# First batch's gate and value from the plain 512-wide read, and weight units in a three-step pipeline with the integer add on DVE

## The chip, the cores and the metric

The kernel runs on one core of a Trainium2 chip. The metric is the device time of one execution in microseconds (us). The engines are named as in the profile: PE is TensorE (matmuls), DVE is VectorE, ACT is ScalarE, POOL is GpSimd, SP is SyncE, which here only issues DMAs. Each engine works its own list of instructions strictly in order and waits on semaphores for the others.

## The reference, cut to what matters

```python
scale = 1.0 / np.sqrt(D)                                        # B, H, S, D = 8, 8, 512, 64; Ns = 32
a = softmax(scale * x @ state.T)                                # per head, over the 32 state rows
xread = a @ state
a2 = softmax(scale * state @ x.T)                               # per head, over the 512 rows
sread = a2 @ x
t = concat([xread, sread])                                      # 8 batches of 512 + 32 rows, 512 wide
g, val = t @ w_gate, t @ w_val                                  # 512 -> 1536
y = (g * sigmoid(g) * val) @ w_out                              # 1536 -> 512
h = y @ w2_in                                                   # 512 -> 2048
out = (h * sigmoid(1.702 * h)) @ w2_out                         # 2048 -> 512
```

## The kernel before

Every product is split in three: each operand is a high part (rounded by a cast) and a low part (the rest), and high x high, high x low and low x high are three matmuls into one PSUM tile. "xh" and "xl" are the two parts of an operand that is read from PSUM: ACT copies the high part, DVE subtracts it.

**Stages.** An opening (the word list START, worked off one word after the other) brings in batch 0's attention and the first weights. Then the blocks of the first expert layer: batches 0 to 6, the "tail" (the 8 x 32 state rows as one block, 256 wide), and batch 7, each as a loop over f = 0..11 (128 columns of the 1536). At last the second layer, nine blocks of 16 steps. All three stages are one list of instructions per engine, in the order in which the code writes them. No scheduler moves anything.

**One f of a block.** The product of the gate (PE, into a PSUM tile gv of which there are two), its sigmoid (ACT, L718), the first multiply (DVE, L720, "mult0"), the product of the value, the second multiply (DVE, L730, "mult1"), the high part of h (ACT, L736), its low part (DVE, L738), and then `out1` of the f before (12 matmuls, L679 to L681). Between them stand pieces of the next batch's attention, at places that the tables BLOCK0 (during batch 0) and GROUP (later) give by f and a place 0, 1 or 2. In all batches the gate's and the value's product goes by `state_weights` and `mm_state`: first the state times the weights of two f (per group of four heads 6 matmuls, then xh and xl of 512 columns), then the attention weights `a` times that, 6 matmuls for each gate and each value. Only the tail takes the plain product, 12 matmuls with the read rows as an operand.

**Weight units.** The weights lie in DRAM as 64-bit floats and come as "units" of 128 x 512 numbers, through four buffers `raw`. A unit is turned into 32-bit floats (`w_begin`): ACT scales the upper word into `wt` and the lower word in place (L192, L193), DVE shifts, and then joins sign and bits (L194, L195), and POOL adds the lower word as integers (L198). Then it is cut (`w_end`): ACT copies the high part (L208), POOL subtracts it (L209). Batch 0 takes 36 such units (24 for gate and value, 12 for out), the tail 4, batch 7 about 24. The out units are stored back as 32-bit floats and from batch 1 on are only cut. In batch 0 `w_beside` puts a begin or an end at five places of each f; elsewhere `need` runs as many as are wanted, with two begun at a time. All weight DMAs are issued on SP.

Of the kernel before, what the change touches and what calls it, by code (L numbers as in the profile page):

```python
# [79 lines left out]
def kernel(  # L80
# [76 lines left out]
    pos = {"dma": 0, "begun": 0, "done": 0, "ahead": 4}  # L157
# [6 lines left out]
    def w_dma(ahead=None):  # L164
        ahead = ahead or pos["ahead"]
        while pos["dma"] < pos.get("limit", len(stream)) and len(raws) + len(held) < ahead:
            key, src, _, _ = stream[pos["dma"]]
            if isinstance(src, tuple):
                raw = work.tile([P, DM], src[0].dtype, name="raw", tag="raw", bufs=RAWS)
                for n, part in enumerate(src):  # L170
                    sy.dma_start(raw[:, n * 2 * P : (n + 1) * 2 * P], part)
            elif src.dtype == F32:
                raw = work.tile([P, DM], F32, name="raw", tag="raw", bufs=RAWS)
                sy.dma_start(raw, src)
            else:
                raw = work.tile([P, DM], src.dtype, name="raw", tag="raw", bufs=RAWS)
                sy.dma_start(raw.rearrange("p (k m) -> p k m", m=src.shape[2]), src)
# [3 lines left out]
    def w_begin():  # L181
# [3 lines left out]
        key, src, _, _ = stream[pos["begun"]]  # L185
        t = raw = raws.pop(key)
        if isinstance(src, tuple) or src.dtype != F32:
# [10 lines left out]
            pool_e.tensor_tensor(tu, tu, lo, op=ALU.add)  # L198
        else:
            held.add(key)  # L200
        temps[key] = t
        pos["begun"] += 1

    def w_end():
        key, src, (pl, tag, bufs), keep = stream[pos["done"]]
        t = temps.pop(key)
        u = (pl or x2p).tile([P, 2, DM], F32R, name="wu", tag=tag, bufs=bufs)
        a.copy(u[:, 0, :], t)  # L208
        pool_e.tensor_tensor(u[:, 1, :], t, f32(u[:, 0, :]), op=ALU.subtract)  # L209
        if keep is not None:  # L210
            sy.dma_start(keep, t)
        held.discard(key)
        units[key] = u
        pos["done"] += 1

    def w_step(lead=2):
        if pos["begun"] > pos["done"]:
            w_end()
# [80 lines left out]
    class Group:  # L299


        def __init__(self, b, g, slots=None):
            self.b, self.g, self.slots = b, g, slots or {}

        def tile(self, tag, shape, dt=F32):
            if tag in self.slots:
                return wp.tile(shape, dt, name=tag, tag=self.slots[tag], bufs=1)
            return ap.tile(shape, dt, name=tag, tag={"aT": "ST", "xth1": "xth0", "xtl1": "xtl0"}.get(tag, tag))
# [12 lines left out]
        def turn(self, q):  # L321
# [6 lines left out]
            self.xt[q] = ps, self.tile(f"xth{q}", [P, S], F32R), self.tile(f"xtl{q}", [P, S], F32R)  # L328
# [515 lines left out]
```

## Time and profile before

| | us |
|---|---|
| median of 3 runs (lowest, highest) | 1674.07 (1673.71, 1675.39) |
| the profiled execution's own time | 1674.44 |
| its span on the core | 1672.7 |
| PE busy in the span | 1568.0 (94%) |
| DVE, ACT, POOL busy | 859.8, 682.1, 350.7 |

The span is what lies between the first and the last instruction; 1.7 us of the time lie around it. The share of busy time mixes stages that have different limits, so the views below are read by stretch. The rows name tiles without their buffer numbers, and an arrow in brackets says how long an engine stood idle before the instruction and whose end it waited for.

### The profile page before, as it was taken

Reading aid. Unit: us, or ns where it says so; the run is one execution under the profiler, and the core shown is the slowest. Engines: PE = TensorE matmul, PEld = TensorE weight load, DVE = VectorE, ACT = ScalarE, POOL = GpSimd, SP = SyncE. Lnnn points to the kernel's source line nnn. Section 1 sums busy time; section 2 is a strip of 40 time slices with the busy share of each in tenths; the row PEclk is TensorE's granted clock in tenths of the full one; section 3 lists DMA queues with packets and bytes.
Section 4 is the critical chain, followed back from the end, with each engine's and each line's share of the span. In section 5 each row is a group of like instructions: output and inputs, shape, how many; then the busy total and the mean of one; then the engine's idle time right before and its main releaser. Section 6 shows DMA issues by size and latency. Waiting matters only on the chain.

```text
span 1672.7 us, 18772 instructions
## 1 busy us (share of the span) xinstructions
PE 1568.0 (94%) x7100; PEld 1274.6 (76%) x7100; DVE 859.8 (51%) x1361; ACT 682.1 (41%) x1217; POOL 350.7 (21%) x263
## 2 busy tenths in 40 slices
PE   4667899999999999989987999999999999999997
PEld 2445688888888888869765888888888888888886
DVE  5788766676767666654787333232322322222222
ACT  5566554545555454544565232222222222222222
POOL 3566322222222221225686020000000000000000
PEclk7788899999999999999999999999999999999999
DMA  4445321212122212223445001010101010000000
GB/s 144 126 137 151 103 52 48 77 42 82 49 67 59 64 45 80 52 76 108 145 157 176 19 0 45 7 45 7 41 10 38 13 38 13 32 20 29 10 26 14
DMA packets 85747, 102.40 MB, mean 61 GB/s; under 512 B 44184, under 2 KB 53400, under 8 KB 85656
## 3 DMA queue, kind: packets, MB, share of 16 engines
q1 hardware_dynamic: 85656, 101.21, 20.1%
q8 instruction: 55, 0.90, 0.2%
q14 instruction: 36, 0.29, 0.1%
HBM read 79.69 MB, written 21.50 MB: 60 GB/s over the span
## 4 chain that ended last, share of the span: by engine, by line
PE 45%; DVE 4%; ACT 1%; issue 1%; DMA 0%; DVEq 0%
PE gv L236 8%; PE gv L235 8%; PE gv L234 8%; PE acc L247 7%; PE acc L246 7%; PE acc L248 7%; DVE wt L195 2%; DVE wt L194 1%; ACT wu L208 0%; ACT wt L192 0%; ACT h L736 0%; DVE sg L730 0%; DVE sg L720 0%; DVE xl L571 0%; DMA raw<-in_moe_w_in_dram 0%
## 5 line engine op out<-in xcount | busy, mean ns | idle before, releaser
L805 DVE TENSOR_TENSOR sg<-gv,sg 128x512 f32<-128x512 f32 (+1 forms) x144 | 95.3, 662 | 426.1 <-ACT sg L804 426.1
L804 ACT ACTIVATE sg<-gv 128x512 f32<-128x512 f32 (+1 forms) x144 | 82.6, 574 | 442.1 <-PE gv L236 442.1
L236 PE MATMUL gv<-xl,wu 128*128 128x512 f32 (+1 forms) x576 | 219.5, 381 | 0.0
L235 PE MATMUL gv<-xh,wu 128*128 128x512 f32 (+1 forms) x576 | 219.2, 381 | 0.0
L234 PE MATMUL gv<-xh,wu 128*128 128x512 f32 (+1 forms) x576 | 219.0, 380 | 0.0
L209 POOL TENSOR_TENSOR wu<-raw,wu 128x512 fp32r<-128x512 f32 x96 | 126.0, 1312 | 425.3 <-ACT wu L208 392.9
L247 PE MATMUL acc<-wu,h 128*128 128x512 f32 x544 | 213.2, 392 | 0.0
L246 PE MATMUL acc<-wu,h 128*128 128x512 f32 x544 | 212.9, 391 | 0.0
L248 PE MATMUL acc<-wu,h 128*128 128x512 f32 x544 | 212.1, 390 | 0.0
L241 PE MATMUL gv<-a,xh 128*128 128x512 f32 x384 | 160.6, 418 | 14.9 <-DVE sg L730 10.0
L242 PE MATMUL gv<-a,xl 128*128 128x512 f32 x384 | 157.6, 410 | 16.8 <-DVE xl L571 16.8
L679 PE MATMUL acc<-h,wu 128*128 128x512 f32 (+1 forms) x432 | 167.0, 387 | 4.8 <-ACT h L736 4.8
L680 PE MATMUL acc<-h,wu 128*128 128x512 f32 (+1 forms) x432 | 165.5, 383 | 0.9 <-POOL wu L209 0.9
L681 PE MATMUL acc<-h,wu 128*128 128x512 f32 (+1 forms) x432 | 165.2, 382 | 1.0 <-DVE h L738 0.9
L243 PE MATMUL gv<-a,xh 128*128 128x512 f32 x384 | 156.3, 407 | 0.0
L571 DVE TENSOR_TENSOR h<-sg,h 128x512 fp32r<-128x512 f32 (+1 forms) x144 | 96.4, 670 | 95.4 <-ACT h L570 90.0
L570 ACT CAST h<-sg 128x512 fp32r<-128x512 f32 (+1 forms) x144 | 86.0, 597 | 105.6 <-DVE sg L805 105.6
L234 PEld LDWEIGHTS gv<-xh,wu 128*128 128x128 f32 x576 | 108.5, 188 | 22.3
L235 PEld LDWEIGHTS gv<-xh,wu 128*128 128x128 f32 x576 | 108.2, 188 | 22.2
L236 PEld LDWEIGHTS gv<-xl,wu 128*128 128x128 f32 x576 | 108.3, 188 | 21.8
L720 DVE TENSOR_TENSOR sg<-gv,sg 128x512 f32<-128x512 f32 (+1 forms) x108 | 71.2, 659 | 95.5 <-ACT sg L718 95.1
L246 PEld LDWEIGHTS acc<-wu,h 128*128 128x128 f32 x544 | 102.1, 188 | 22.5
(105 smaller groups left out, 2728.0 us busy)
## 6 DMA issues: line engine op xcount, KB each, us to landing
raw<-w1o SPq DMA_DIRECT2D x96, 256.0 KB
raw<-in_moe_w_out_dram SPq DMA_DIRECT2D x28, 512.0 KB
y<-ev SPq DMA_DIRECT2D x16, 512.0 KB
raw<-in_moe_w_in_dram SPq DMA_DIRECT2D x16, 512.0 KB
xr<-y SPq DMA_DIRECT2D x32, 256.0 KB
out_dram<-ev SPq DMA_DIRECT2D x16, 512.0 KB
xn<-in_x_dram SPq DMA_DIRECT2D x14, 512.0 KB
raw<-in_moe_w_gate_dram SPq DMA_DIRECT2D x24, 256.0 KB
```

The costliest lines, as they stand in the source:

```text
L234: pe.matmul(ps[:, :N], wh, xh, start=k == 0, stop=False)
L235: pe.matmul(ps[:, :N], wl, xh, start=False, stop=False)
L236: pe.matmul(ps[:, :N], wh, xl, start=False, stop=k == KD - 1)
L241: pe.matmul(ps, wh, xh, start=k == 0, stop=False)
L242: pe.matmul(ps, wl, xh, start=False, stop=False)
L243: pe.matmul(ps, wh, xl, start=False, stop=k == len(pairs) - 1)
L246: pe.matmul(ps, lh, rh, start=first, stop=False)
L247: pe.matmul(ps, lh, rl, start=False, stop=False)
L248: pe.matmul(ps, ll, rh, start=False, stop=last)
L679: pe.matmul(ps, w[:, 0, c], h[:, 0, :N], start=f == 0, stop=False)
L680: pe.matmul(ps, w[:, 1, c], h[:, 0, :N], start=False, stop=False)
L681: pe.matmul(ps, w[:, 0, c], h[:, 1, :N], start=False, stop=f == F1 - 1)
```

## The change

Four things are changed. Batch 0's gate and value take the plain product: the read rows (`xread`, the softmax weights stacked as high and low part in `stk`, times the state's two parts) become the operand `xop`, and each gate and value is 12 matmuls; there is no `state_weights` in batch 0. The weight units go through a pipeline (`w_slot`): one slot turns unit n on ACT, copies the high part of a unit joined in an earlier slot, joins unit n on DVE, and subtracts the low part of the one copied. The integer add (L208 of after) is DVE's, in `w_join`, as an instruction that the listing of the order calls ISA, with 128x1024 as its shape. In batch 0 three slots stand in each f (`beside`), their subtractions in turn on POOL and on DVE; elsewhere `need` runs slots with the subtraction on POOL. The first four units' eight DMAs are issued on ACT's queue ahead of all else there. The scores of the first two groups are computed for two heads' pairs at once (`scores_wide`).

```diff
 START = """
-A0.load0 state0 A0.load1 weights1 A0.turn0 A1.load0 attn_state A0.turn_h0 A1.load1 weights2 A0.turn1
...
+weights4 A0.load0 state0 A0.load1 A1.load0 A1.load1 A0.turn0 attn_state A0.turn_h0 A0.turn_l0:v A0.turn1
+slot A0.turn_h1 A0.turn_l1:v A0.scores_wide A1.turn0 slot A0.max_n A1.turn_h0 A0.less_max:p A1.turn_l0:v
+A1.turn1 A0.exp_n A1.turn_h1 A1.turn_l1:v A1.scores_wide A0.sum_n cut_state A0.over_sum:v slot A0.back
+A1.max_n A0.stack_h0:a A0.stack_l0:v A0.stack_h1:a A0.stack_l1:v xread0 xread1 A1.less_max:v A1.exp_n slot
+xread_l0 xread_l1 A1.sum_n A1.over_sum:v A1.back A0.max_s A1.stack_h0:a A1.stack_l0:v A1.stack_h1:a
+A1.stack_l1:v xread2 xread3 slot A1.max_s xread_l2 xread_l3 G0.load A1.exp_s A0.exp_s state1
...
-    pos = {"dma": 0, "begun": 0, "done": 0, "ahead": 4}
+    pos = {"dma": 0, "turned": 0, "joined": 0, "cut": 0, "ahead": 4, "q": a}
...
+    def w_join():
+        t, hi, lo = temps[stream[pos["joined"]][0]]
+        pos["joined"] += 1
+        if hi is not None:
+            tu = t.bitcast(U32)
             v.tensor_scalar(out=tu, in0=tu, scalar1=3, scalar2=None, op0=ALU.logical_shift_left)
             v.scalar_tensor_tensor(
                 out=tu, in0=hi, scalar=0x80000000, in1=tu, op0=ALU.bitwise_and, op1=ALU.bitwise_or
             )
-            pool_e.tensor_tensor(tu, tu, lo, op=ALU.add)
...
+            v.tensor_tensor(tu, tu, lo, op=ALU.add)
+
+    def w_slot(eng=None):
+
+        if pos["turned"] < pos["dma"]:
+            w_turn()
+        key, src, (pl, tag, bufs), keep = stream[pos["cut"]]
+        ready = pos["cut"] < pos["joined"] and pos["cut"] < pos.get("cap", len(stream))
+        if ready:
+            t = temps.pop(key)[0]
+            u = (pl or x2p).tile([P, 2, DM], F32R, name="wu", tag=tag, bufs=bufs)
+            a.copy(u[:, 0, :], t)
+        if pos["joined"] < pos["turned"]:
+            w_join()
+        if ready:
+            (eng or pool_e).tensor_tensor(u[:, 1, :], t, f32(u[:, 0, :]), op=ALU.subtract)
...
     def need(key):
-        while pos["done"] <= where[key]:
-            w_step()
+        while pos["cut"] <= where[key]:
+            w_slot()
...
+    def xread(hp):
+        ps = at()
+        stk, sb = stks.pop(hp)[0], stks["state"]
+        pe.matmul(ps, sb[:, 0, hp, :], stk, start=True, stop=False)
+        pe.matmul(ps, sb[:, 1, hp, :], stk, start=False, stop=True)
+        xop[hp] = x_tiles(xp, hp, S)
+        a.copy(xop[hp][0], ps)
+        return lambda: v.tensor_tensor(xop[hp][1], ps, f32(xop[hp][0]), op=ALU.subtract)
...
+        plain = tail or i == 0
...
-            for g, place in enumerate([(F1 - 1, 1)] * 2 if tail else [(F1 - 2, 1), (F1 - 1, 0)]):
+            for g, place in enumerate([(F1 - 1, 1)] * 2 if plain else [(F1 - 2, 1), (F1 - 1, 0)]):
...
+        def beside():
+
+            if i == 0:
+                w_slot(v if pos["cut"] % 2 else pool_e)
...
             product(pg, f, 0)
+            beside()
             sg = work.tile([P, 512], F32, name="sg", tag="sg")
             a.activation(sg[:, :N], pg[:, :N], ACTF.Sigmoid)
-            w_beside("B")
             v.tensor_tensor(sg[:, :N], pg[:, :N], sg[:, :N], op=ALU.mult)
-            w_beside("E")
...
             product(pv, f, 1)
-            w_beside("B")
+            beside()
             v.tensor_tensor(sg[:, :N], pv[:, :N], sg[:, :N], op=ALU.mult)
...
                 out1(f - 1, nxt, 0) if f == F1 - 1 else out1(f - 1)
+            beside()
             run(f, 2)
```

In the listings below, L720/L730/L738 of before are L775/L784/L790 of after, L194/L195 are L204/L205, and the cut L208/L209 of before is L219/L223.

DVE in batch 0, f = 3, from mult0 to the last row before the next mult0. Before:

```order
L720 TENSOR_TENSOR sg_667<-gv_660,sg_667 128x512
L345 TENSOR_TENSOR ST_673<-at_674,ST_673 64x512
L335 TENSOR_TENSOR xtl1_685<-at_679,xth1_684 128x512
L194 TENSOR_SCALAR wt_695<-wt_695 128x512
L195 SCALAR_TENSOR_TENSOR wt_695<-raw_522,wt_695 128x512
L730 TENSOR_TENSOR sg_667<-gv_688,sg_667 128x512
L194 TENSOR_SCALAR wt_708<-wt_708 128x512
L195 SCALAR_TENSOR_TENSOR wt_708<-raw_575,wt_708 128x512
L738 TENSOR_TENSOR h_717<-sg_667,h_717 128x512
L194 TENSOR_SCALAR wt_736<-wt_736 128x512
L195 SCALAR_TENSOR_TENSOR wt_736<-raw_596,wt_736 128x512
L571 TENSOR_TENSOR xl_752<-at_744,xh_751 128x512
```

After, the same step (the slot that stands before the next mult0 with it):

```order
L775 TENSOR_TENSOR sg_680<-gv_656,sg_680 128x512
L362 TENSOR_TENSOR ST_683<-at_684,ST_683 64x512
L352 TENSOR_TENSOR xt1_694<-at_689,xt1_694 128x512
L204 TENSOR_SCALAR wt_710<-wt_710 128x512
L205 SCALAR_TENSOR_TENSOR wt_710<-raw_552,wt_710 128x512
L208 ISA wt_710<-raw_552,wt_710 128x1024
L784 TENSOR_TENSOR sg_680<-gv_697,sg_680 128x512
L790 TENSOR_TENSOR h_723<-sg_680,h_723 128x512
L204 TENSOR_SCALAR wt_738<-wt_738 128x512
L205 SCALAR_TENSOR_TENSOR wt_738<-raw_593,wt_738 128x512
L208 ISA wt_738<-raw_593,wt_738 128x1024
L223 TENSOR_TENSOR wu_741<-wt_710,wu_741 128x512
```

The three units of a step stay; each has one instruction more on DVE, every second low part is DVE's, and the low part `xl` of `state_weights` is gone.

ACT in the tail, its first two f, with the one 64-bit unit (wt_6292 before, wt_6333 after). Before:

```order
L718 ACTIVATE sg_6280<-gv_6267 128x256
L208 CAST wu_6283<-raw_6009 128x512
L192 ACTIVATE wt_6292<-raw_6286 128x512
L193 ACTIVATE raw_6286<-raw_6286 128x512
L736 CAST h_6314<-sg_6280 128x256
L718 ACTIVATE sg_6330<-gv_6317 128x256
```

After:

```order
L774 ACTIVATE sg_6288<-gv_6275 128x256
L219 CAST wu_6291<-raw_6017 128x512
L789 CAST h_6314<-sg_6288 128x256
L774 ACTIVATE sg_6330<-gv_6317 128x256
L192 ACTIVATE wt_6333<-raw_6294 128x512
L193 ACTIVATE raw_6294<-raw_6294 128x512
```

The turn of this unit stands one f later, behind h of f = 0 and the sigmoid of f = 1; on DVE its join stands likewise behind mult0 of f = 1.

ACT in batch 7, one f from sigmoid to sigmoid. Before:

```order
L718 ACTIVATE sg_7546<-gv_7539 128x512
L208 CAST wu_7549<-raw_7412 128x512
L192 ACTIVATE wt_7554<-raw_7486 128x512
L193 ACTIVATE raw_7486<-raw_7486 128x512
L570 CAST xh_7577<-at_7570 128x512
L736 CAST h_7581<-sg_7546 128x512
L208 CAST wu_7584<-wt_7525 128x512
L208 CAST wu_7599<-wt_7554 128x512
L192 ACTIVATE wt_7602<-raw_7531 128x512
L193 ACTIVATE raw_7531<-raw_7531 128x512
L718 ACTIVATE sg_7617<-gv_7610 128x512
```

After (`L219 CAST wu_7678<-wt_7655` copies the unit whose turn stands three rows above it):

```order
L774 ACTIVATE sg_7617<-gv_7610 128x512
L622 CAST xh_7627<-at_7620 128x512
L192 ACTIVATE wt_7631<-raw_7558 128x512
L193 ACTIVATE raw_7558<-raw_7558 128x512
L219 CAST wu_7634<-raw_7516 128x512
L789 CAST h_7652<-sg_7617 128x512
L192 ACTIVATE wt_7655<-raw_7560 128x512
L193 ACTIVATE raw_7560<-raw_7560 128x512
L219 CAST wu_7658<-wt_7631 128x512
L219 CAST wu_7678<-wt_7655 128x512
L622 CAST xh_7681<-xr_7537 128x512
L774 ACTIVATE sg_7692<-gv_7685 128x512
```

The two cuts of an f now stand behind the second turn, and the second of them cuts the unit that was turned just before it, ahead of the next sigmoid.

## Rows read from the trace of the kernel before

**Rows 1.** The page's 40 slices of the span: busy tenths of PE.

```profile
PE   4667899999999999989987999999999999999997
```

**Rows 2.** Stretches: length; busy us (count) of PE, PEld, DVE, ACT, POOL; PEclk; DMA.

```profile
0.00:42.00 42.00, 20.04 (x64) 11.58 (x64) 24.07 (x42) 21.28 (x37) 12.55 (x15) 0.80 0.50 144
42.00:167.00 125.00, 85.37 (x319) 62.68 (x320) 103.07 (x153) 79.43 (x144) 76.64 (x56) 0.84 0.46 138
167.00:201.00 34.00, 26.01 (x100) 19.27 (x99) 25.28 (x43) 16.96 (x29) 12.01 (x9) 0.85 0.27 75
...
740.00:760.00 20.00, 14.11 (x101) 13.64 (x100) 7.04 (x14) 7.88 (x17) 6.39 (x5) 0.83 0.43 145
...
805.00:920.00 115.00, 95.98 (x378) 72.15 (x377) 91.67 (x106) 71.05 (x130) 84.70 (x61) 0.96 0.54 169
```

**Rows 3.** Groups by line and shape, 42 to 167 us: DVE, POOL, one of PE.

```profile
L195 DVE SCALAR_TENSOR_TENSOR wt<-raw,wt 128x512 uint32<-128x512 uint32 x29 | 26.7, 922 | 1.1
L194 DVE TENSOR_SCALAR wt<-wt 128x512 uint32<-128x512 uint32 x28 | 23.8, 850 | 11.1 <-ACT wt L192 10.9
L370 DVE TENSOR_TENSOR xc<-xn,xc 128x512 fp32r<-128x512 f32 x6 | 8.7, 1491 | 0.0
...
L198 POOL TENSOR_TENSOR wt<-wt,raw 128x512 uint32<-128x512 uint32 x29 | 40.4, 1392 | 46.4 <-DVE wt L195 18.3 <-issue 6.6 <-ACT wt L192 6.1
...
L242 PE MATMUL gv<-a,xl 128*128 128x512 f32 x36 | 18.1, 503 | 13.6 <-DVE xl L571 13.6
```

**Rows 4.** Timeline of DVE: start, duration, instruction, idle before it (opening, then f = 4).

```profile
2.63 0.91 DVE L274 MEMSET stz<- 128x1024 f32 x1 [0.16 <-issue]
...
12.81 0.43 DVE L194 TENSOR_SCALAR wt<-wt 128x512 uint32<-128x512 uint32 x1 [2.19 <-ACT wt L192]
13.27 0.69 DVE L195 SCALAR_TENSOR_TENSOR wt<-raw,wt 128x512 uint32<-128x512 uint32 x1
13.88 0.70 DVE L377 STREAM_TRANSPOSE sp<-ST 128x512 f32<-128x512 f32 x1
...
41.97 0.68 DVE L720 TENSOR_TENSOR sg<-gv,sg 128x512 f32<-128x512 f32 x1
...
97.93 1.63 DVE L195 SCALAR_TENSOR_TENSOR wt<-raw,wt 128x512 uint32<-128x512 uint32 x1
...
166.89 0.68 DVE L720 TENSOR_TENSOR sg<-gv,sg 128x512 f32<-128x512 f32 x1
```

**Rows 5.** Timeline of PE in batch 0, around a wait.

```profile
127.38 0.80 PE L242 MATMUL gv<-a,xl 128*128 128x512 f32 x1 [4.04 <-DVE xl L571]
127.97 0.63 PE L243 MATMUL gv<-a,xh 128*128 128x512 f32 x1
128.40 0.63 PE L241 MATMUL gv<-a,xh 128*128 128x512 f32 x1
...
130.46 0.39 PE L243 MATMUL gv<-a,xh 128*128 128x512 f32 x1
130.69 0.39 PE L679 MATMUL acc<-h,wu 128*128 128x512 f32 x1
```

**Rows 6.** Timeline in the tail: ACT, PE.

```profile
749.42 0.66 ACT L192 ACTIVATE wt<-raw 128x512 f32<-128x512 f32 x1 [5.60 <-DMA raw<-in_moe_w_in_dram]
...
751.65 0.58 PE L241 MATMUL gv<-xh,wu 128*128 128x256 f32 x1 [5.89 <-DVE sg L730]
```

**Rows 7.** Groups by line and shape, 805 to 920 us (batch 7): DVE, ACT.

```profile
L195 DVE SCALAR_TENSOR_TENSOR wt<-raw,wt 128x512 uint32<-128x512 uint32 x25 | 38.6, 1545 | 0.9
L194 DVE TENSOR_SCALAR wt<-wt 128x512 uint32<-128x512 uint32 x25 | 18.2, 729 | 11.4 <-ACT wt L192 11.4
...
L736 ACT CAST h<-sg 128x512 fp32r<-128x512 f32 x12 | 7.5, 622 | 36.0 <-DVE sg L730 36.0
```

**Rows 8.** Timeline of DVE in batch 7: mult1 of two f.

```profile
861.72 0.68 DVE L730 TENSOR_TENSOR sg<-gv,sg 128x512 f32<-128x512 f32 x1
...
870.36 0.68 DVE L730 TENSOR_TENSOR sg<-gv,sg 128x512 f32<-128x512 f32 x1
```

More of the change, by code (lines that the diff above doesn't have):

```diff
@@ L197, in w_begin @@
             )
-            pool_e.tensor_tensor(tu, tu, lo, op=ALU.add)
[L199 to L218, printed above, removed]
+            v.tensor_tensor(tu, tu, lo, op=ALU.add)
[12 more added lines that the diff above has]
+            (eng or pool_e).tensor_tensor(u[:, 1, :], t, f32(u[:, 0, :]), op=ALU.subtract)
+            if keep is not None:
+                sy.dma_start(keep, t)
+            held.discard(key)
+            units[key] = u
+            pos["cut"] += 1
         w_dma()
-        while pos["begun"] < min(pos["done"] + lead, len(stream)):
-            w_begin()
-            w_dma()
     def need(key):
-        while pos["done"] <= where[key]:
-            w_step()
+        while pos["cut"] <= where[key]:
+            w_slot()
     def mm_in(ps, w, xop, N, ks=range(KD)):
@@ L307, in tile, with half @@
                 return wp.tile(shape, dt, name=tag, tag=self.slots[tag], bufs=1)
-            return ap.tile(shape, dt, name=tag, tag={"aT": "ST", "xth1": "xth0", "xtl1": "xtl0"}.get(tag, tag))
+            return ap.tile(shape, dt, name=tag, tag={"aT": "ST", "xt1": "xt0"}.get(tag, tag))
+        def half(self, first, second):
+            tag = second or first
+            if first not in self.slots:
+                return self.tile(tag, [P, S])
+            if first not in self.both:
+                self.both[first] = self.tile(first, [P, 2, S])
+            return self.both[first][:, int(second is not None)]
         def load(self, q=None):
@@ L475, in state_weights @@
         for q in range(2):
-            sh, sl = (stz[b % 2][:, g, i + q : i + q + 2].rearrange("p c m -> p (c m)") for i in (1, 5))
+            sh, sl = groups[b, g].columns(q)
             w = units["gv", u, 2 * g + q]
@@ L601 @@
         "attn_state": lambda: attn_state(0),
-        "begin": w_begin,
-        "end": w_end,
-        "sw0": lambda: state_weights(0, 0, 0),
-        "sw1": lambda: state_weights(0, 0, 1),
-    }
+        "cut_state": cut_state,
+        "slot": w_slot,
+    }
+    for hp in range(HP):
+        more[f"xread{hp}"] = lambda hp=hp: xread_first(hp)
+        more[f"xread_l{hp}"] = lambda hp=hp: lows.pop(hp)()
     for b in range(2):
@@ L650 @@
         pos["limit"] = where["o", 1, 2] if i == 0 else len(stream)
+        pos["cap"] = where["o", 1, 0] if i == 0 else len(stream)
         if blk + 1 < B:
@@ L707, in coming @@
             u = f // 2 + 1
-            if u < U1 and not tail:
-                need(("gv", u, 2 * g + 1))
+            if u < U1 and not plain:
                 state_weights(blk, u, g)
```

107 lines of the change are left out of this document (58 added, 49 removed).

## The prediction

> **What bounds the kernel now.** I read the slices of the page first: PE stands at 9 tenths nearly everywhere, below it only in the first four slices, around the eighteenth and in the slices behind the twentieth [rows 1]. The table by stretch says how much room each of these places has [rows 2]: PE is busy 20.0 of the first 42 us, 85.4 of 125 from the first mult0 of batch 0 to its tenth, 26.0 of 34 in the end of batch 0, 14.1 of 20 in the tail and 96.0 of 115 in batch 7. All else is PE work that the change leaves as it is, so only these places can move. In batch 0 the busiest engine beside PE is DVE, 103.1 of 125 us, with POOL at 76.6. The groups say why [rows 3]: the two DVE instructions of a unit take 0.92 and 0.85 us on average, where the same two take 0.69 and 0.43 in the opening when POOL is quiet [rows 4]; one at 97.93 took 1.63. PE waits there for the low part of state_weights (13.6 us before L242), which stands on DVE behind such units.
>
> First what the numbers are set against: the profiled execution took 1674.4, 0.4 above the median of 1674.07.
>
> **The join on DVE.** A unit's shift and join take DVE from one start to the next 0.46 and 0.61 us (12.81, 13.27, 13.88 in [rows 4]). The integer add is not in this trace. It cannot be free, since it is one more instruction in DVE's order. As one pass over two inputs of 512 it would cost the 0.61 of L195; if it goes twice over them, as its listed shape of 1024 could mean, 1.22. The one row with 1024 elements is the memset of 0.91 [rows 4], and starts follow each other a little faster than durations say; I take **0.85**, a join of 1.92, and keep 0.61 to 1.22 for the range. What leaves is POOL's add, 1.39 us each [rows 3].
>
> [...]
>
> **The opening (+5).** The first mult0 stands at 41.97 [rows 4]. DVE gets six adds (5.1), four xl of xread instead of two of state_weights (+1.2), the state's cut (0.6) and four half-height low parts of the stack instead of two low parts of a (+0.4): 7.3 us more, in a stretch in which DVE is busy only 24.1 of 42 [rows 2]. The path also gets longer by the read, which now lies between the softmax and the first product, and ACT first issues eight weight DMAs, of which the last four wait for the first to land; its turns and casts are queued behind those. Between 0 (all of it falls into idle time) and 9, I take 5.
>
> **Batch 0, first to tenth mult0 (-9.6).** Now 166.89 - 41.97 = 124.9 us [rows 4]. DVE's 103.1 without the units' 26.7 + 23.8 is 52.6; nine xl of state_weights (0.68 each) go, 46.5 stay, and of those L370 is stretched by 6 x (1.49 - 0.69) = 4.8 [rows 3], so that 41 to 42 are work. After: 27 joins x 1.92 = 51.8, 14 low parts on DVE x 0.61 = 8.5, the rest 41: 101.3. To that come stretches. Today they are 29 x 0.23 + 28 x 0.42 + 4.8 = 23.3 us beside 56 POOL instructions, 0.42 each; 14 POOL subtractions remain, 6 us at that rate and 13 at the most (1.63 against 0.69 each); I take 7. Idle time is 22 us now, 11.1 of it for ACT's turn, which hangs on POOL; in the new order the turn is queued behind no instruction that waits for POOL's add. I leave 7 for the sigmoids. Sum 115.3.
>
> What hides PE's extra work: 72 state_weights matmuls become 144 more in the products, so an f has 36 with out1, 8.4 us at the 0.23 us of the high clock (130.46 to 130.69) and 15.5 at the 0.43 of the low one (127.97 to 128.40, behind a wait of 4.04) [rows 5]. With 12.8 us a step this is covered at the high clock and not at the low one.
>
> **The end of batch 0 (-4.9).** From the tenth mult0 to 201 are 34 us [rows 2, 4]. DVE has three joins left (5.8), and PE 96 matmuls x 0.23 = 22.4 behind that mult0, with reads and transposes some 24. I take 29, between that floor and today's.
>
> **The tail (-5).** ACT waits 5.60 us for a unit's DMA, DVE stands behind that turn with mult1, and PE idles 5.89 [rows 6] and then runs some 13 matmuls of 256 columns at the low clock (0.83 granted in the stretch [rows 2]; half of 0.43 against half of 0.23 each, 1.3 us): 7 us. In the new order the turn and its join stand behind the sigmoid and mult0 of the next f. PE then has 36 more matmuls of 256 columns (0.12 each) before it needs the mult1 behind the join: from 751.65 - 5.89 = 745.8 to about 750.1, while that join is done at 749.42 + 0.57 + 1.92 = 751.9. About 2 us of idling stay. Between 0 and -7, I take -5.
>
> **Batch 7 (+9).** Here the rhythm is a chain: mult1 to mult1 is 8.64 us [rows 8], and ACT idles 36.0 us before its 12 copies of h [rows 7]. The new chain: sigmoid 0.7, mult0 0.6, join 1.92, mult1 0.7, h 0.5, turn 0.65, join 2.0, copy of that very unit 0.55 (ACT's next sigmoid is queued behind it, and PE's product behind that), 7.65; the copies and low parts for state_weights and the second layer add 0.5 on average: 8.2. Today's stretches are 25 x 0.86 + 25 x 0.30 = 29 us beside 61 POOL instructions [rows 2, 7], 0.47 each; of five an f three remain, 1.4 us. That is 9.6 an f against 8.7 or so, twelve times 0.8 or 0.9, hence about 10; some of the subtractions fall beside the multiplies, which read PSUM and are not stretched, so 9. The ends are 8.2 (-6 in all) and, with 1.0 for each subtraction, 11.2 (+30).
>
> Batches 1 to 6 cut stored units only and have PE full; the two 64-bit units of the second layer have DVE and POOL idle around them: nothing.
>
> **The sum.** 5 - 9.6 - 4.9 - 5 + 9 = -5.5, 1674.4 - 5.5 = 1668.9, and 0.4 less as a median: **1668**.
>
> **The rivals.**
> *Slower: the last batch's lock.* In batch 7 the add lengthens the time in which DVE has two SBUF inputs, and each of the three subtractions an f is released by a copy just when a join starts. If each costs the full 1.63 - 0.69, about 1.0, an f lasts 11.2 and the whole comes to 1668 + 21 = 1689. For it speaks that L195 there takes 1545 ns on average and is stretched nearly every time [rows 7]; against it that POOL has three instructions instead of five. It makes the kernel slower than now once an f exceeds 10.2 us.
>
> [...]
>
> *Slower: a long add.* At 1.22 the 57 joins that lie on a path (27, 6 and 24) cost 0.37 more each, 21 us: 1689. Nothing in the trace speaks for it but the listed 1024.
>
> *PE keeps batch 0.* If PE goes on in bursts with waits of over 2.6 us, half of its 36 matmuls an f run at the low clock: 12 us and a transposition or read, 13.3 against 13.9 now. The batch then gains 5 instead of 14.5 and the whole stays at about 1677: no change. For it speaks the granted clock of 0.84 [rows 2].
>
> *Faster: POOL's stretches vanish.* With half of the subtractions on DVE and none of the adds on POOL the stretches and the idle time of batch 0 could come to 4 in place of 14 (-20), the opening's work could fall into idle time (+2), and batch 7 stay as it is: with -4.9 and -5 it gives about 1646. For it speaks that the idle time of today hangs on POOL; against it that the sigmoids still wait for PE.
>
> That the change does not do what it says is small: the order shows the instructions where the words put them.
>
> **How the numbers follow.** The forecast with its neighbourhood (1660 to 1671) has 0.37, the faster rival 0.15, PE keeping batch 0 0.17, the lock in batch 7 0.19, the long add 0.12. A measurement of this kernel can tell about 0.2% (3.3 us) from no change. Faster: the forecast's 0.37 and the faster rival's 0.15, and 0.01 from the others, 0.53. Within 0.2%: 0.17. Slower: the two slower rivals less 0.01, 0.30. The range leaves out half of the faster rival (below 1647) and a third to a half of the two slower ones (above 1689): 1647 to 1689.
>
> **What would show it.** The add's row: 0.6 to 0.9 us, or over 1.1. The tenth mult0 at 162 or earlier, with the first near 47. The end of batch 0 at about 191. In the tail no wait of PE over 3 us. In batch 7, mult1 to mult1: 9.6 as summed, 8.2 without stretches, over 10.2 with the lock. If the first batch gains less than 5 or batch 7 moves by less than 2, a term of the sum is wrong even where the total fits.

## The result, and the profile after

The changed kernel takes 1697.01 us (1696.28 to 1697.66) against 1674.14, a ratio of 1.0135 with the interval 1.0118 to 1.0153: slower by 22.9 us, where the forecast's terms added up to 5.5 less (1668) and the range ended at 1689. The span of its profile is 1695.2, 22.5 above that of before.

The first multiply of an f (mult0, L720 before, L775 after) marks the stages in both traces. "Opening" is the start of the first mult0 of all, "batch 0" the time from the first to the tenth, "end" from there to batch 1's first, "tail" from its first to batch 7's first, and "batch 7" the mean distance of its twelve; all in us. The runs of the next section stand in the same table.

| kernel | time | opening | batch 0 | end | tail | batch 7 |
|---|---|---|---|---|---|---|
| before | 1674.1 | 42.0 | 124.9 | 36.2 | 62.6 | 8.73 |
| after | 1697.0 | 60.6 | 112.7 | 35.5 | 62.5 | 10.27 |
| e1_sp_dma | 1692.3 | 55.7 | 112.6 | 36.6 | 61.4 | 10.27 |
| e2_no_add | 1622.2 | 51.5 | 88.6 | 32.0 | 57.2 | 7.41 |
| e3_lag | 1688.8 | 60.5 | 112.7 | 35.5 | 66.8 | 9.36 |
| e4_late_old | 1682.5 | 61.0 | 112.6 | 36.5 | 63.5 | 8.76 |
| e5_start | 1688.8 | 50.7 | 112.3 | 35.3 | 62.6 | 10.27 |
| e6_dve_sub | 1678.8 | 60.0 | 112.7 | 33.9 | 59.3 | 8.84 |
| e7_pool_add | 1671.5 | 55.6 | 104.6 | 35.1 | 57.7 | 9.58 |
| e8_mix | 1655.5 | 51.1 | 98.2 | 32.9 | 62.8 | 8.75 |
| e9_before_dve_add | 1701.5 | 44.5 | 132.8 | 36.3 | 65.9 | 10.01 |
| e10_no_pool | 1675.3 | 54.9 | 111.0 | 35.0 | 60.6 | 8.84 |
| e11_mix_slots | 1644.5 | 51.0 | 96.9 | 32.9 | 64.0 | 7.85 |
| e12_mix_old | 1641.9 | 51.4 | 98.1 | 32.7 | 62.8 | 7.62 |
| e13_less_v | 1641.1 | 50.3 | 98.1 | 32.9 | 63.0 | 7.58 |
| e14_start_order | 1645.4 | 53.4 | 100.4 | 32.8 | 62.9 | 7.58 |

From before to after the marks move by +18.7 at the end of the opening, then by -12.3 and -0.7 in batch 0, by +0.6 from there to the end of the tail (the tail alone -0.2) and by +15.9 in batch 7 (its end included): 22.2. Batches 1 to 6 and the second layer don't move: the shift is 5.7 us at every mult0 from the second of batch 1 to the last of batch 6, and 22.2 at all of the second layer.

After, the table by stretch at those marks (length; busy us and count of PE, PEld, DVE, ACT, POOL; granted clock; DMA share, GB/s), which answers to [rows 2]: opening, batch 0, its end, tail, batch 7.

```profile
0.00:61.00 61.00, 24.01 (x63) 15.47 (x64) 36.30 (x55) 24.95 (x44) 8.66 (x12) 0.97 0.38 108
61.00:173.00 112.00, 89.54 (x371) 69.64 (x371) 103.90 (x181) 72.20 (x131) 17.36 (x13) 0.92 0.50 154
173.00:209.00 36.00, 32.27 (x142) 26.21 (x141) 26.48 (x50) 17.92 (x32) 2.59 (x2) 0.95 0.25 80
749.00:812.00 63.00, 59.03 (x444) 57.12 (x443) 31.46 (x54) 24.27 (x54) 20.50 (x16) 0.95 0.33 108
812.00:938.00 126.00, 96.52 (x357) 72.10 (x356) 102.41 (x128) 69.95 (x127) 46.41 (x36) 0.92 0.45 143
```

In the opening PE does little more than before, in 19 us more. In batch 0 DVE is busy 103.9 of 112: it sets the pace. In batch 7 PE idles nearly 30 us, with DVE busy 102.4 of 126.

The units' instructions after, by line and shape (busy us, mean ns; idle before them and who ended it), over the opening and batch 0 (0 to 190 us), and over batch 7 (811 to 941 us), which answers to [rows 3, 7]:

```profile
L208 DVE CUSTOM_DVE_ANT_0 wt<-raw,wt 128x1024 uint16<-128x1024 uint16 x36 | 34.4, 956 | 5.3 <-DVE wt L205 0.5
L205 DVE SCALAR_TENSOR_TENSOR wt<-raw,wt 128x512 uint32<-128x512 uint32 x36 | 28.0, 777 | 1.2
L204 DVE TENSOR_SCALAR wt<-wt 128x512 uint32<-128x512 uint32 x36 | 17.1, 474 | 8.5 <-ACT wt L192 8.4
...
L223 POOL TENSOR_TENSOR wu<-wt,wu 128x512 fp32r<-128x512 f32 x20 | 26.9, 1343 | 153.0 <-ACT wu L219 135.1 <-DVE wt L205 17.9
```

```profile
L208 DVE CUSTOM_DVE_ANT_0 wt<-raw,wt 128x1024 uint16<-128x1024 uint16 x25 | 36.2, 1447 | 3.8 <-DVE wt L205 0.5
L205 DVE SCALAR_TENSOR_TENSOR wt<-raw,wt 128x512 uint32<-128x512 uint32 x25 | 21.4, 858 | 0.9
...
L219 ACT CAST wu<-wt 128x512 fp32r<-128x512 f32 x24 | 14.7, 614 | 22.2 <-DVE wt L208 22.2
L789 ACT CAST h<-sg 128x512 fp32r<-128x512 f32 x12 | 7.4, 620 | 31.3 <-DVE sg L784 31.3
```

The integer add is L208, listed as 1024 words of 16 bits. It takes 1447 ns on average in batch 7. What it takes alone, and what meets it, is seen in the timeline: DVE at 16 to 22 us and POOL beside it, then one f of batch 7 with ACT and POOL.

```profile
15.78 0.69 DVE L205 SCALAR_TENSOR_TENSOR wt<-raw,wt 128x512 uint32<-128x512 uint32 x1
16.61 0.69 DVE L208 CUSTOM_DVE_ANT_0 wt<-raw,wt 128x1024 uint16<-128x1024 uint16 x1
...
21.28 1.65 DVE L208 CUSTOM_DVE_ANT_0 wt<-raw,wt 128x1024 uint16<-128x1024 uint16 x1
...
21.10 1.28 POOL L223 TENSOR_TENSOR wu<-wt,wu 128x512 fp32r<-128x512 f32 x1 [19.80 <-ACT wu L219]
```

```profile
879.68 0.61 ACT L219 CAST wu<-wt 128x512 fp32r<-128x512 f32 x1
...
880.36 1.29 POOL L223 TENSOR_TENSOR wu<-wt,wu 128x512 fp32r<-128x512 f32 x1 [4.35 <-ACT wu L219]
...
880.56 1.64 DVE L208 CUSTOM_DVE_ANT_0 wt<-raw,wt 128x1024 uint16<-128x1024 uint16 x1
...
882.23 0.62 ACT L219 CAST wu<-wt 128x512 fp32r<-128x512 f32 x1 [1.95 <-DVE wt L208]
...
883.38 0.69 DVE L775 TENSOR_TENSOR sg<-gv,sg 128x512 f32<-128x512 f32 x1 [1.18 <-ACT sg L774]
```

Alone the add is 0.69 us, and it starts 0.83 behind L205. Beside POOL's subtraction it ends 0.55 us after that has ended (21.10 + 1.28 = 22.38, and 22.93; in batch 7 881.65, and 882.20). The subtraction is not there by chance: the copy of the slot (L219, 879.68) releases it just when the join of the same slot reaches its add. So 20 of the 25 adds of batch 7 and four of their L205 take over 1.5 us, and one add 1.27, each beside a subtraction; in the opening five of the six adds take over 1.5. ACT's next copy then waits 1.95 for that add, the sigmoid stands behind the copy, and mult0 waits for the sigmoid.

The trace of before shows the same meeting, with L195 in the add's place (POOL and DVE in batch 7, before):

```profile
859.78 1.48 POOL L209 TENSOR_TENSOR wu<-raw,wu 128x512 fp32r<-128x512 f32 x1
862.03 1.30 POOL L198 TENSOR_TENSOR wt<-wt,raw 128x512 uint32<-128x512 uint32 x1 [0.78 <-DVE wt L195]
...
860.14 1.67 DVE L195 SCALAR_TENSOR_TENSOR wt<-raw,wt 128x512 uint32<-128x512 uint32 x1
861.72 0.68 DVE L730 TENSOR_TENSOR sg<-gv,sg 128x512 f32<-128x512 f32 x1
862.32 0.68 DVE L571 TENSOR_TENSOR xl<-at,xh 128x512 fp32r<-128x512 f32 x1
```

L195 ends 0.55 after the subtraction L209 (861.26, and 861.81). In batch 7 of before 22 of the 25 L195 are long, 21 of them by a subtraction alone. Only one of the 25 adds on POOL (L198) stands beside an L195; about half of their time (some 17 of 33.9 us) they stand beside L720, L730 and the L571 of `at`, each of which reads one input from PSUM, and these keep their 0.68 to 0.69.

### The profile page after: what moved, and what is told of

It is laid out like the page before. It is cut to its first block, busy times and chain, and to the rows that moved or that the text cites. A ratio compares the mean times of both kernels' runs of the same rounds, so it can differ in the third digit from the quotient of the medians.

```text
span 1695.2 us, 18900 instructions
## 1 busy us (share of the span) xinstructions
PE 1587.4 (94%) x7180; PEld 1295.5 (76%) x7180; DVE 893.6 (53%) x1440; ACT 679.6 (40%) x1210; POOL 230.2 (14%) x179
## 4 chain that ended last, share of the span: by engine, by line
PE 45%; DVE 5%; ACT 1%; issue 1%; DVEq 0%; ACTq 0%
PE gv L243 7%; PE gv L242 7%; PE gv L241 7%; PE acc L254 7%; PE acc L253 7%; PE acc L255 7%; DVE wt L208 2%; DVE wt L205 1%; DVE wt L204 1%; DVE sg L775 0%; ACT h L789 0%; DVE sg L784 0%; DVE h L790 0%; DVE xl L623 0%; ACT sg L774 0%
## 5 line engine op out<-in xcount | busy, mean ns | idle before, releaser
L223 POOL TENSOR_TENSOR wu<-raw,wu 128x512 fp32r<-128x512 f32 x96 | 124.1, 1293 | 466.7 <-ACT wu L219 434.3
L248 PE MATMUL gv<-a,xh 128*128 128x512 f32 x336 | 137.5, 409 | 23.7 <-DVE sg L784 14.6
L623 DVE TENSOR_TENSOR h<-sg,h 128x512 fp32r<-128x512 f32 (+1 forms) x144 | 95.5, 663 | 95.5 <-ACT h L622 90.1
L250 PE MATMUL gv<-a,xh 128*128 128x512 f32 x336 | 134.6, 401 | 0.0
L249 PE MATMUL gv<-a,xl 128*128 128x512 f32 x336 | 134.6, 400 | 0.0
L241 PEld LDWEIGHTS gv<-xh,wu 128*128 128x128 f32 x576 | 108.4, 188 | 22.2
L775 DVE TENSOR_TENSOR sg<-gv,sg 128x512 f32<-128x512 f32 (+1 forms) x108 | 71.4, 661 | 94.5 <-ACT sg L774 94.0
L253 PEld LDWEIGHTS acc<-wu,h 128*128 128x128 f32 x544 | 102.1, 188 | 22.5
```

Of the source, the lines that this page charges most:

```text
L241: pe.matmul(ps[:, :N], wh, xh, start=k == 0, stop=False)
L248: pe.matmul(ps, wh, xh, start=k == 0, stop=False)
L249: pe.matmul(ps, wl, xh, start=False, stop=False)
L250: pe.matmul(ps, wh, xl, start=False, stop=k == len(pairs) - 1)
L253: pe.matmul(ps, lh, rh, start=first, stop=False)
```

## The experiments

Theory L: the add's move to DVE is the loss, by its own time and by POOL's hold on it. The rivals: the transfers' order (D) in the opening, the order of the copies in batch 7 (C), the slots or the plain read in themselves (P).

**e1_sp_dma.** First weights on SP, behind the first loads of x and state.

```diff
-weights4 A0.load0 state0 A0.load1 A1.load0 A1.load1 A0.turn0 ...
+A0.load0 state0 A0.load1 weights1 A1.load0 A1.load1 weights4 A0.turn0 ...
...
-    pos = {..., "q": a}
+    pos = {..., "q": sy}
```

> The changed kernel with the first weights' DMAs issued on SP behind the first x and state loads, as before the change; nothing else. Theory D (the opening is late because eight weight transfers go ahead of x and state): the first three transpositions on PE stand at 4.5, 5.7 and 8.2 us again instead of 8.5, 11.8 and 13.2, the first mult0 at about 55 instead of 60.6, and the whole at 1691 instead of 1697. Rival L (the opening is a chain of DVE instructions that POOL stretches, and has slack ahead of it): the transpositions come earlier, but the weights now come later and mult0 stays within 2 us of 60.6; the whole 1695 to 1697.

1692.3, with the first mult0 at 55.7: D holds for 4.9 of the opening's 18.7. In the changed kernel PE waited for x and state, and SP's issue of the four state loads took 6.51 us, beside ACT's eight, where it takes 2.04 in e1; PE's first transposition stands at 8.47, where it stood at 4.50 before (here PE, then SP's queue, of after):

```profile
8.47 1.08 PE L341 MATMUL at<-ident,xn 128*128 128x128 f32 x4 [8.47 <-DMA sb_raw<-in_state_dram]
11.81 1.09 PE L297 MATMUL at<-ident,sb_raw 128*128 128x128 f32 x4 [2.25 <-DMA xn<-in_x_dram]
...
2.15 6.51 SPq L289 DMA_DIRECT2D sb_raw<-in_state_dram  x4
```

**e2_no_add.** `v.tensor_tensor(tu, tu, lo, op=ALU.add)` is left out.

> The changed kernel with the integer add left out, so that a unit lacks its lower word; all else as it is. It measures what the add costs in each place, with what POOL adds to it. Theory L (each add costs its own 0.83 us and, nearly always beside a subtraction of POOL, 0.8 to 1.0 more): opening 7 to 9 us less (first mult0 near 52), batch 0 from first to tenth mult0 15 to 20 less than 112.7, batch 7 from 10.3 to about 8 us an f (25 us less), the whole about 1650. Rival C (the add itself is nearly hidden and the order of the copies is what costs): batch 7 stays above 9.3 us an f, the opening above 57, the whole 1675 to 1685.

1622.2: 75 us less, more than L said. Opening -9.1, batch 0 -24.0, end -3.5, tail -5.3, batch 7 -2.9 an f. In batch 0 PE and DVE are then both busy 81 of the 88 us from 52 to 140. So the add, with all that it drags along, is more than three times the whole loss. This kernel does less work than either of the two, so it doesn't say what the other parts of the change are worth; e7 does.

**e3_lag.** The copy of a unit one slot later in the tail and in batch 7.

```diff
-        ready = pos["cut"] < pos["joined"] and ...
...
+        behind = 0 if idle else pos.get("lag", 0)
+        ready = pos["cut"] < pos["joined"] - behind and ...
```

> The changed kernel with the copy of a unit one slot later in the tail and in batch 7, so that ACT copies a unit that was joined a slot earlier and not the one just turned. Theory C (batch 7 is slow because the copy ahead of the sigmoid waits for its own unit's join, 22.2 us of ACT's idle time there): that wait goes, batch 7 falls from 10.3 to 8.6 to 9.0 us an f, the whole to about 1680. Theory L (DVE's joins, stretched by POOL's subtractions, fill the cycle): ACT's wait only moves to the h copies, batch 7 stays above 9.8 us an f and the whole at 1692 to 1697.

Between both: 9.36 us an f, 1688.8. ACT's wait of 22.2 is gone, but the wait for mult1 grew from 31.3 to 42.6, and the add still takes 1180 ns. Batch 7 takes 10 us less; the tail takes 4.3 more, and that the later copies of its few units are the cause was not tried apart.

```profile
L221 ACT CAST wu<-wt 128x512 fp32r<-128x512 f32 x24 | 14.7, 612 | 0.0
L796 ACT CAST h<-sg 128x512 fp32r<-128x512 f32 x12 | 7.4, 620 | 42.6 <-DVE sg L791 42.6
```

**e4_late_old.** From batch 1 on the old begin and end, the add on POOL.

```diff
+        while pos["turned"] < min(pos["cut"] + lead, len(stream)):
+            w_turn()
+            w_join(pool_e)
+            w_dma()
```

> The changed kernel up to the end of batch 0, and from batch 1 on the units as before the change: two begun at a time, a unit begun and another ended in turn, the integer add on POOL. Expected by the stage marks, whatever the mechanism: tail and batch 7 as before the change (batch 7 8.7 us an f), so that 16 to 17 of the 22.9 us go, 1680 to 1681, and 5.7 us stay from batch 0. If it stays above 1685, what was read as batch 7's loss hangs on something else than the units' pipeline (the clock, or the place of the transfers).

1682.5, and 8.76 us an f as before the change: the loss in batch 7 is the units' pipeline, its order and the add's place together. The whole stays 1.5 above what was expected; in the profile the end of batch 0 is 1.0 longer than after's and the tail 1.1.

**e5_start.** e1, and the add on POOL for the opening's units alone.

```diff
-    pos = {..., "q": a}
+    pos = {..., "add": pool_e, "q": sy}
...
-            v.tensor_tensor(tu, tu, lo, op=ALU.add)
+            pos["add"].tensor_tensor(tu, tu, lo, op=ALU.add)
...
     extra.clear()
+    pos["add"] = v
```

> The changed kernel with the first weights' transfers on SP behind x and state, and with the integer add of the opening's units alone on POOL (later units as changed). Theory L for the opening (an add on DVE costs 0.83 us and, with POOL's subtraction beside it, 0.95 more, on a chain that has no slack): first mult0 at 48 to 50 us instead of 55.7, the whole at about 1686. Rival (the add's place doesn't matter, since a later slot's subtraction on POOL then waits for POOL's add): first mult0 stays at 54 to 56, the whole at 1691 to 1693.

The first mult0 at 50.7, 5.0 less than in e1: L holds, with a smaller size than expected. The whole falls by 3.5 only: in this profile batch 6 is 2.8 longer than after's (92.9, 90.1), which no run explains.

**e6_dve_sub.** All subtractions of the tail and of batch 7 on DVE.

```diff
-            (eng or pool_e).tensor_tensor(u[:, 1, :], ...)
+            (eng or pos.get("sub", pool_e)).tensor_tensor(u[:, 1, :], ...)
...
+        if i >= NB1 - 2:
+            pos["sub"] = v
```

> The changed kernel with every subtraction of the tail and of batch 7 on DVE, so that POOL has nothing there. If POOL's subtractions are what stretches the adds in batch 7 (L208 1447 ns on average against 0.69 us alone), L208 falls to 0.69 us throughout, DVE gets three subtractions of 0.61 us an f, and these cancel most of the 1.9 us won: 9.4 to 10.3 us an f instead of 10.3, the whole 1686 to 1698. If the stretch has another cause, L208 stays above 1.2 us and batch 7 comes to over 11.5 us an f, the whole to over 1710.

1678.8. With POOL empty the add is 693 ns in all 25 cases, so POOL's subtraction is the stretch; DVE does 36 instructions more and an f is yet 1.43 us shorter, better than expected: from the first to the last mult0 of batch 7 DVE idles 9 us there, 22 in the changed kernel, so that a good part of the subtractions fills idle time. The groups of batch 7 there:

```profile
L208 DVE CUSTOM_DVE_ANT_0 wt<-raw,wt 128x1024 uint16<-128x1024 uint16 x25 | 17.3, 693 | 3.4
L205 DVE SCALAR_TENSOR_TENSOR wt<-raw,wt 128x512 uint32<-128x512 uint32 x25 | 17.3, 693 | 0.9
...
L219 ACT CAST wu<-wt 128x512 fp32r<-128x512 f32 x24 | 14.7, 614 | 10.9 <-DVE wt L208 10.9
```

**e7_pool_add.** The add on POOL everywhere, the rest as changed.

```diff
-            v.tensor_tensor(tu, tu, lo, op=ALU.add)
+            pool_e.tensor_tensor(tu, tu, lo, op=ALU.add)
```

> The changed kernel with the integer add back on POOL everywhere, the order of the slots and all else as changed: the plain read and the pipeline without the add's move. Theory L (the move of the add is the loss): opening 52 to 55 us, first to tenth mult0 of batch 0 95 to 105 instead of 112.7, batch 7 8.3 to 9.3 us an f, the whole 1660 to 1675. Rival P (the slots' order or the plain read is the loss): batch 7 stays above 10 us an f and the opening near 60, the whole above 1690.

1671.5, 0.9985 of before (0.9975 to 0.9994). The change without the add's move is a small gain, 2.5 us. But batch 7 takes 9.58 us an f, more than L's 8.3 to 9.3: here C is right, ACT's copies wait 31.6 us for POOL's adds of the units just joined.

```profile
L219 ACT CAST wu<-wt 128x512 fp32r<-128x512 f32 x24 | 14.7, 615 | 31.6 <-POOL wt L208 31.6
```

**e8_mix.** e1 and e4, the add on POOL in batch 0 too, and all of batch 0's subtractions on DVE.

```diff
-                w_slot(v if pos["cut"] % 2 else pool_e)
+                w_slot(v)
```

> Plain read and slots in batch 0 with the add on POOL and all of batch 0's subtractions on DVE (a unit then costs DVE 1.07 + 0.61 us, POOL 1.3), first transfers on SP, and from batch 1 on the units as before the change. By the stages: opening 48 to 51, first to tenth mult0 95 to 105, end of batch 0 about as before, tail and batch 7 as before: 1674 + 7 - 25 = 1656, between 1650 and 1665. If POOL's add now meets DVE's subtractions as the subtraction met the add, the first to tenth mult0 stay above 110 us and the whole comes to over 1668.

1655.5, as summed: batch 0 in 98.2 and the late blocks as before. It beats both kernels (0.9887 of before, 0.9873 to 0.9902).

**e9_before_dve_add.** The kernel before, with its L198 on `v` instead of `pool_e`.

> The kernel before with one line changed: the integer add on DVE instead of POOL; its order, its state_weights and all else as they were. Theory L (the move of the add is a loss in itself: 0.83 us on DVE and a stretch by each of POOL's remaining subtractions, for 1.39 us of POOL that nobody waits for): opening 45 to 47 us, first to tenth mult0 of batch 0 125 to 135, batch 7 9.2 to 10.2 us an f, the whole 1685 to 1700. Rival (the add's place is harmless where the old order stands, only the slots make it a loss): batch 7 at or under 8.8 us an f, the whole at or under 1676.

1701.5, 26.8 more than before: the add's move alone costs more than the whole change. Batch 0 is 7.9 longer, batch 7 1.28 an f. In batch 7 the add takes 1136 ns on average, and L195 still 1082, beside POOL's 36 subtractions:

```profile
L198 DVE CUSTOM_DVE_ANT_0 wt<-raw,wt 128x1024 uint16<-128x1024 uint16 x25 | 28.4, 1136 | 3.4
L195 DVE SCALAR_TENSOR_TENSOR wt<-raw,wt 128x512 uint32<-128x512 uint32 x25 | 27.1, 1082 | 0.9
```

**e10_no_pool.** e1, and every subtraction of a unit on DVE; the add stays on DVE.

```diff
-            (eng or pool_e).tensor_tensor(u[:, 1, :], ...)
+            (eng or v).tensor_tensor(u[:, 1, :], ...)
...
-                w_slot(v if pos["cut"] % 2 else pool_e)
+                w_slot(v)
```

> The changed kernel with the first transfers on SP and with every subtraction of a unit on DVE, so that the add stays on DVE and POOL has no part in the units. If what the add costs is mostly POOL's hold on DVE, L208 is 0.69 us everywhere, the opening 51 to 52 us instead of 55.7, first to tenth mult0 105 to 111 instead of 112.6, batch 7 8.8 us an f, the whole 1660 to 1672. If it is mostly the add's own time, DVE now carries 0.61 us more a unit and gains nothing: batch 0 stays at or over 112 us and the whole over 1675.

1675.3, neither of the two: the add is 693 ns everywhere and batch 7 8.84, but the opening is 54.9 and batch 0 111.0. In batch 0, where DVE has little idle time (busy 103.3 of 111), the subtractions' own 0.61 on DVE cost nearly what the hold had cost; where it has some, as in batch 7, the hold was the dearer one. Batches 1 to 5, whose stored units are now cut on DVE too, take 0.9 more each.

**e11_mix_slots and e12_mix_old.** Both take batch 0 as in e8, with the subtractions of the tail and of batch 7 on DVE. e11 keeps the slots with the later copy of e3; e12 keeps the old begin and end (here the line of e8's `w_end` that it changes).

```diff
-        pool_e.tensor_tensor(u[:, 1, :], t, f32(u[:, 0, :]), op=ALU.subtract)
+        (v if pos["old"] > 1 else pool_e).tensor_tensor(u[:, 1, :], t, f32(u[:, 0, :]), op=ALU.subtract)
```

> Slots everywhere, the add on POOL and the subtractions of batch 0, the tail and batch 7 on DVE, first transfers on SP, and in the tail and batch 7 the copy one slot later. Batch 0 as in the run that mixed old and new (98 us from first to tenth mult0). In batch 7 DVE has 2 x 1.07 + 3 x 0.61 for units and POOL two adds an f, and ACT waits for neither: 7.9 to 8.6 us an f instead of 8.75, the whole 1645 to 1655; the tail may lose 4 as it did with the later copy. If the hold that counts is the one of POOL's adds, batch 7 stays at 8.7 to 9.5 and the whole at 1655 to 1664.

> As the run that mixed old and new (plain read and slots in batch 0 with the add on POOL, units of later batches begun and ended as before the change), with the subtractions of the tail and of batch 7 on DVE too. POOL keeps two adds of five instructions an f: DVE loses about three stretches of 0.5 to 0.9 us and gets three subtractions of 0.61: 8.2 to 9.0 us an f instead of 8.75, the whole 1649 to 1659.

1644.5 with 7.85 us an f, and 1641.9 with 7.62, both better than expected; in batch 7 of e12 L205 falls to 692 ns (L195's 1545 in [rows 7]). e12 is 0.9802 of before (0.9787 to 0.9816): adds on POOL, subtractions on DVE.

**e13_less_v and e14_start_order.** What is left of the opening: e12 with one word changed, and e12 with its words in another order.

```diff
-A0.less_max:p
+A0.less_max:v
```

```diff
+A0.turn_h1 A0.turn_l1:v A0.scores_wide A1.turn0 slot cut_state A0.max_n A0.less_max:v A0.exp_n A1.turn_h0
+A1.turn_l0:v A1.turn1 A1.turn_h1 A0.sum_n A0.over_sum:v A0.back A1.turn_l1:v A1.scores_wide slot
...
+A1.sum_n A1.over_sum:v A1.back xread_l0 xread_l1 A1.stack_h0:a A1.stack_l0:v A1.stack_h1:a
```

> The last version (old units from batch 1 on with late subtractions on DVE) with one word of the opening changed: the first group's less_max on DVE, not behind an add and a subtraction on POOL. Of the 9.5 us by which the first mult0 there (51.4) is still later than before (42.0), theory O (the words' order makes the first softmax wait behind units) gives this place 2 to 3: first mult0 at 48.5 to 49.5, the whole 2 to 3 less than 1641.9. Rival R (the read's own path sets it: stack, xread, xl, 12 matmuls a product at the low clock, all behind the second group) says that the second group's softmax, not the first's, ends the chain: mult0 within 1 us of 51.4.

> The last version with the opening's words in another order, the same work: both groups' softmax pieces ahead of the units' slots where they can be, the state's cut early, both less_max on DVE. Theory O: first mult0 at 45 to 48, the whole 1636 to 1639. Rival R: the path of the read is what is left, mult0 at 50 or later, and the whole within 2 us of 1641.9.

1641.1 with mult0 at 50.3, and 1645.4 with 53.4. Neither theory is met in full: O's mult0 is too early in both runs; R misses by 0.1 in e13's mult0 and by 1.5 in e14's whole. In e13 the first group's softmax is done 1.1 earlier than in e12 (start of its last transposition), and mult0 comes 1.1 earlier. In e14 it is done at 20.6 instead of 26.5, the second group's at 37.5 instead of 38.7, and mult0 still comes later. So what is won at the first group need not reach mult0.

Of the 9.5 us by which e12's mult0 is later than before, 2.5 stand ahead of the second group's first transposition (27.1, before 24.6), 4.1 between its first and its last (11.6, before 7.6), and 2.9 from there to mult0 (12.7, before 9.8). The 4.1 are in the trace: DVE makes the stack's low parts and two low parts of the read, and ACT copies the read, within that softmax; its exponential starts at 32.56, right behind those copies, where it stood at 27.26 before (DVE and ACT of e12).

```profile
28.51 1.93 DVE L469 TENSOR_TENSOR stk<-aT,stk 64x512 fp32r<-64x512 f32 x2
34.84 1.28 DVE L541 TENSOR_TENSOR xl<-at,xh 128x512 fp32r<-128x512 f32 x2
...
31.95 0.59 ACT L540 CAST xh<-at 128x512 fp32r<-128x512 f32 x1 [0.27 <-PE at L538]
32.56 0.63 ACT L439 ACTIVATE ST<-ST 128x512 f32<-128x512 f32 x1
```

In e14, where the second group's exponential stands ahead of the read, that stretch is 8.7, but 15.9 pass from its end to mult0. What the read costs once it is placed best stays open; the wide scores, which all these runs have too, were not tried apart.

## Why the prediction failed, point by point

Four of the five terms were too low: the opening by 13.7 us, batch 7 by 6.9, the tail by 5.6 (with the 0.7 of the batches ahead of it), the end of batch 0 by 4.2. Batch 0 was 2.7 better than forecast. Two steps carry most of it: the opening's term, which took DVE's idle time for room and left the transfers out, and the price of what POOL adds to DVE's instructions, which was an average over two kinds of which only one mattered.

- **The join: right by luck, and yet the wrong price.** It was put at 1.92 from start to start, and alone it is 0.46 + 0.83 + 0.61 = 1.90. But 0.61 was taken from L205 to the add, where it is 0.83, and 0.85 for the add, where it is 0.61: two errors that cancel. The long add (rival, 1.22) did not come true.
- **What POOL adds: the step that failed.** The forecast divided the stretches by all POOL instructions, 0.47 us each over batch 7's 61, and kept that price for the 36 subtractions that remain. Nearly all of L195's stretches, 25 x (1.545 - 0.69) = 21 us, came from these 36 subtractions, 0.59 each; the 25 adds that left were hardly a part of it (the other 8 us of the forecast's 29, L194's, stood beside both kinds and did go). After, the add and L205 pay 25 x (1.447 - 0.69) + 25 x (0.858 - 0.69) = 23 us for the same 36, 0.64 each, where 12 x 1.4 = 17 were summed. So the meetings went on, and the add's own time came on top. In e6, with POOL empty, both are 0.69 and an f is 1.43 us shorter, though DVE does the subtractions too.
- **Batch 7 (+9; measured +15.9).** The chain was named rightly, with the copy that waits for its own unit. 10.27 us an f is the rival of the lock, just over the 10.2 from which it was to decide; it lies between the forecast's 9.6 and that rival's 11.2, since about two of three subtractions an f meet an add or L205 (25 of 36). e6 takes 1.43 away by emptying POOL, e3 0.9 by the later copy. A single meeting says more here than the trace's average of 0.47: an add took 1.65 beside POOL's 1.28, and 693 ns with POOL empty (e6).
- **The opening (+5; measured +18.7).** The largest miss, outside the "0 to 9" given for it. 4.9 are the transfers (e1), which were listed in the sentence and then not summed. 5.0 are the add (e5, against e1): its six cost 8.8 us on DVE and not 5.1, since five are stretched. Some 9 stay in every version with the plain read; e12's trace shows where they stand, and no run what would remove them. The bound "up to 9" was a count of DVE's work, not of the chain: the opening is a sequence of waits between ACT, DVE, PE and POOL, so work added to it isn't swallowed by idle time elsewhere in the same 42 us. Even the count was low: the four half-height low parts take 0.69 each, no less than full ones (L445, 64x512, 687 ns on average).
- **Batch 0 (-9.6; measured -12.3).** Right in mechanism and near in size: DVE sets the pace, 103.9 of 112 us busy, with 8.7 us of stretches where 7 were taken. The rival that PE keeps batch 0 did not come: the granted clock rose from 0.84 to 0.92, and PE has three waits of over 2.6 us there (3.13 to 4.74), where before it had six (2.63 to 6.81); behind each, matmuls of 512 columns stand 0.43 apart, the low clock of [rows 5].
- **The end of batch 0 (-4.9; measured -0.7)** was a guess between two ends, and the lower one was wrong: PE's floor of 24 us counted 96 matmuls, but up to batch 1's first mult0 stand 139, of which 123 have 512 columns (before 111 in all, since a gate or value then took half as many). PE is busy 31.7 of the 35.5 us there, so that at most 3.8 could go; the versions with the add on POOL and the subtractions on DVE take 32.7 to 32.9.
- **The tail (-5; measured +0.6).** e7 with POOL's add has the 5 us (57.7). In the changed kernel the join behind the late DMA is stretched, so PE idles 3.41 and not 2 (5.89 before), and then runs at the low clock for 5.7 us, to 765.6, where it was 3.3 before (751.65 to 755.0). From batch 6's last mult0 to batch 7's first PE idles 5.2 us in all (6.4 before), and some 11 more matmuls at the low clock, 0.09 us dearer each, take 1.0 of that back (ACT, DVE and PE of after, to be read against [rows 6]):

```profile
755.85 0.68 ACT L192 ACTIVATE wt<-raw 128x512 f32<-128x512 f32 x1 [3.17 <-DMA raw<-in_moe_w_in_dram]
...
757.85 1.69 DVE L208 CUSTOM_DVE_ANT_0 wt<-raw,wt 128x1024 uint16<-128x1024 uint16 x1
...
759.93 0.58 PE L248 MATMUL gv<-xh,wu 128*128 128x256 f32 x1 [3.41 <-DVE sg L784]
...
765.43 0.41 PE L249 MATMUL gv<-xh,wu 128*128 128x256 f32 x1
...
765.79 0.28 PE L248 MATMUL gv<-xh,wu 128*128 128x256 f32 x1
```

- **The sum.** e9 (the add alone, +26.8) and e7 (all but the add, -2.5) make 24.3, close to the 22.9 measured. The sign was lost on that one part, the add's move. Two slips of the working are small: 34.1 to 29 is 5.1 and not 4.9, and the terms of batch 7's chain add up to 7.62 and not 7.65. How much of e7's gain in batch 0 is the plain read's and how much the slots' was not tried apart.

## What to carry to other kernels

Before work is moved to the busier of two engines, ask who waits for it where it is: in the kernel before, ACT's copies waited for nine of POOL's 68 adds, 11.7 us in all and none in batch 7, while the same add on DVE stood ahead of the copies, multiplies and products that set the pace. When two engines hold each other up, don't spread the cost over all their instructions: see in the trace which kind stands beside which. Here the subtractions met DVE's joins and the adds mostly did not, so moving the adds away freed little; the adds on POOL and the subtractions on DVE (e12) took 2% off the time before. In an opening without a bound engine, follow the chain of waits; a count of one engine's work says little.

## What the runs showed of the hardware that was not expected

The integer add on DVE, listed as 1024 words of 16 bits, takes 0.69 us, the same as L205, which is listed as 512 words of 32 bits (0.69). Its distance to the next start is 0.61 (16.61 to 17.22 in after), so the 1.22 of two passes was not seen.

Beside a subtraction on POOL, 21 of the 22 long L195 of batch 7 before and the 21 adds of batch 7 after that met one, all with both inputs in SBUF, ended 0.54 to 0.56 us after it. The multiplies L720 and L730, which read one input from PSUM, never took more than 0.694 us in the trace of before, though POOL was at work beside 100 of their 192 instructions of 512 columns.

And the low clock behind a wait lasted very unequally: some 3 us behind a wait of 4.04 in batch 0 (127.38 to 130.46 in [rows 5]), 5.7 us behind one of 3.41 in the tail (759.93 to 765.6, above).
